# A fused attention and two-MoE kernel: 32-bit low words, fewer filler products, another table of urgencies

## The chip, the cores and the metric

The kernel runs on one core of a Trainium2 chip. A core has TensorE (PE in the profile, with PEld for its weight loads), VectorE (DVE), ScalarE (ACT), GpSimd (POOL) and SyncE (SP), which here issues all transfers. The metric is the device time of one execution in microseconds; lower is better.

## The reference

Three stages follow each other. The first is an attention of 4 batches, 8 heads, 576 tokens and head size 64 (a band of seven neighbours, plus an attention on tokens averaged by four); its result is a matrix x of 2304 tokens by 512. Two layers with weights follow:

```python
x = transpose(attn_out).reshape(2304, 512)
x = ((x @ w_a) * (x @ w_b)) @ w_out          # d_ff 1536
h = x @ w_in2                                # d_ff 2048
g = maximum(h, 0) + alpha * minimum(h, 0)
out = (g @ w_out2).astype(float32)
```

The weights arrive in eight bytes each (float64 bits); q, k, v are float32.

## The kernel before

Every matmul of the layers uses fp16 pairs: a number is split into a high and a low fp16 word after scaling by a power of two, and three products (high·high, high·low, low·high) are added in PSUM.

The work is cut into steps: `s1(j, f)` makes the 128 hidden columns f of layer 1 for the 288 tokens of block j (24 products of 288 columns, into two of the four PSUM banks m0 to m3), `s2(j, d)` the second half of layer 1 (36 products), `s3` and `s4` the same for layer 2 in blocks of 384 tokens. Blocks 0 and 1 of s1 are interleaved, four steps to each chunk of weights; block 1 needs tile 5, the last of batch 0. The PE steps of s1 to s4 form one chain with a fixed order. Around the chain lie the attention tiles (`turn`, `soft`, `p_turn`, `av_t`, 24 of them; `x_add` writes a tile's fp16 pair into xt) and the preparation of the weights, all on shared buffers: the tile zone holds attention data first and weights of layer 2 later, wo and x2s hold raw weights first.

After each s1 step ACT copies one bank to tm, DVE multiplies it with the other bank (`tm<-m,tm`), ACT makes the high word (`gt<-tm`) and DVE the low one (`gt<-gt,tm`); s2 reads gt. After s2, DVE adds two banks into x2s (`x2s<-m,tm`).

`narrow` turns a raw tile of eight-byte weights into float32 in four passes: ACT scales the low 32-bit word of each weight to a small count and writes it back over the raw tile, DVE puts two bits of the top word beside it (in the orders `TENSOR_SCALAR wo<-wo` or `zone<-zone`, 16-bit), DVE shifts the high word into the destination (`TENSOR_SCALAR wab<-wo`), and POOL adds the two. `cols_bound` (ACT), `top_of` (PE, DVE: tr, td) and `cols_split` (ACT and DVE, after us_ab and ws) then give scaled fp16 pairs. There are 48 raw tiles: 20 of 1024 weights per partition (12 of w_a and w_b, 8 of w_in) and 28 of 512 (w_out of both layers). Raw tiles of w_a and w_b are loaded into three places in turn.

A planner sets the order of every engine's instructions before anything is issued. `Plan.cost` gives each instruction an estimated duration, `reschedule` runs a list schedule in which the ready instruction of highest urgency goes first, and the table URGENT shifts the urgency of groups of steps by hand. `fill` then looks at each gap that the plan shows on PE in its first 200 us and puts constant products (identity by identity, 128x256, `m<-idf`) into 0.7 of it. An engine runs its instructions strictly in the issued order.

Of the kernel before, what the change touches and what calls it, by code (L numbers as in the profile page):

```python
# [12 lines left out]
U32 = mybir.dt.uint32  # L13
# [12 lines left out]
class Plan:  # L26
# [66 lines left out]
    def cost(self, eng, method, out, ins, kw):  # L93
        n = self.free(out)
        if eng == self.PE:
            if method == "transpose":
                n = self.free(out)
                w = 2 if ins[0].dtype == F32 else 1
            else:
                w = 4 if ins[0].dtype == F32 else 1  # L100
            return max(0.03, n * w * 0.000425)
        m = max([n] + [self.free(a) for a in ins])
        if eng == self.POOL:
            return 0.2 + m * (0.0026 if method == "tensor_tensor" else 0.0011)
        if eng == self.ACT:
            if ins and ins[0].dtype == U32:
                return 0.2 + 0.00243 * m
            return 0.2 + 0.0009 * m + (0.19 if kw.get("accum_out") is not None else 0)
        if out.dtype == I16:
            return 0.1 + 0.00144 * m  # L110
        if method in ("tensor_scalar", "tensor_copy", "memset", "tensor_scalar_mul"):
            return 0.12 + 0.0009 * m
        return 0.14 + 0.0011 * m
# [130 lines left out]
    def fill(self, t0, t1, chain, early, stat, mov, each):  # L244


        pe = [o for o in self.order if o.eng == self.PE]
        f = self.nc.tensor.matmul
        add = []
        for a, b in zip(pe, pe[1:]):  # L250
            n = int(0.7 * (b.start - a.end) / each)
            if n < 2 or not t0 <= a.end < t1:
                continue
            g = next(o for o in chain if o.start >= b.start)
            if g is chain[0]:
                out = early
            else:
                if not g.calls[0][2]["start"] or any(p.end > a.end - 0.5 for p in g.preds if p.eng in (self.DVE, self.ACT)
                                                     and p.name[:2] in ("s1", "s2")):
                    continue  # L260
                out = g.calls[0][1][0]
            o = self.new(self.PE)
            o.calls = [(f, (out[:, :mov.shape[1]], stat, mov), dict(start=True, stop=True))] * n
            o.start, o.end = a.end + 1e-6, b.start
            o.name, o.n = "fill", -1
            add.append(o)
        self.order = sorted(self.order + add, key=lambda o: o.start)
# [11 lines left out]
def kernel(  # L279
# [24 lines left out]
    def V(method, *a, **kw):  # L304
        P("vector", method, *a, **kw)

    def A(method, *a, **kw):
        P("scalar", method, *a, **kw)

    def G(method, *a, **kw):  # L310
        P("gpsimd", method, *a, **kw)
# [151 lines left out]
    def narrow(raw, dst):  # L463


        w = raw.bitcast(I32).rearrange("p (n t) -> p n t", t=2)
        h = raw.bitcast(I16).rearrange("p (n t) -> p n t", t=4)
        A("activation", out=h[:, :, 0], in_=raw.bitcast(U32).rearrange("p (n t) -> p n t", t=2)[:, :, 0],
          func=ACTF.Copy, scale=2.0 ** -29)
        V("tensor_scalar", out=h[:, :, 1], in0=h[:, :, 3], scalar1=-0x4000, scalar2=None, op0=ALU.bitwise_and)  # L470
        d = dst.bitcast(I32)
        V("tensor_scalar", out=d, in0=w[:, :, 1], scalar1=3, scalar2=0x3FFFFFFF,
          op0=ALU.logical_shift_left, op1=ALU.bitwise_and)
        G("tensor_tensor", out=d, in0=d, in1=w[:, :, 0], op=ALU.add)
# [20 lines left out]
    def rows_narrow(t, i, n, raw):  # L495
        narrow(raw, slot(t, i))
        A("activation", out=raw.bitcast(BF16)[:, :DM], in_=slot(t, i), func=ACTF.Square, accum_out=row_ss[n][:, i:i + 1])
# [17 lines left out]
    def cols_words(t, i, raw):  # L515
        narrow(raw, slot(t, i))
# [646 lines left out]
    for n, i in enumerate((3, 4, 5)):  # L1163
        t = head_end + 4 * n
# [36 lines left out]
    for i in range(3, NTILE):  # L1201
        b, t = divmod(i, TPB)
# [37 lines left out]
    def group(name):  # L1240
        kind = name.rstrip("0123456789")
        n = name[len(kind):]
        if kind in ("turn", "bound", "soft", "pturn", "av", "v", "x", "load") and n:
            b = int(n) // TPB
            return f"{kind}@{b}" if kind in ("x", "load") else f"t@{b}" if b else f"t0@{n}"
        if name[:3] in ("s1_", "s2_"):
            return f"{name[:2]}@{name[3]}"
        return kind if kind in ("wow", "wos", "wo2w", "wo2s") else name


    URGENT = {"alphas": -35, "bs0": -60, "bs1": -115, "bs2": 15, "bs3": -25, "gexp0": -45, "gexp1": -90,
# [13 lines left out]

    cal.sort(key=lambda x: x[:2])
    for _, _, fn, P.name, bias, P.rel in cal:
        P.bias = bias + URGENT.get(group(P.name), 0.0)
        fn()
# [35 lines left out]
```

## Time and profile before

| | us |
|---|---|
| median of 3 runs (lowest to highest) | 1039.46 (1034.23 to 1042.77) |
| the profiled execution | 1042.84 |
| span in the profile, first to last instruction | 1041.1 |
| PE busy, share of the span | 1004.1, 96% |
| DVE busy | 611.7, 59% |
| ACT busy | 512.1, 49% |
| POOL busy | 140.4, 13% |

The profiled execution took 1.7 us more than its span and is the slowest of the four times. Constant products count as PE busy, so PE's 96% is more than its useful share.

### The profile page before, as it was taken

How to read it: one execution, taken by the hardware profiler on the slowest of the kernel's cores; microseconds unless marked ns; L12 is line 12 of the kernel's file. 1: busy time of each engine (PE TensorE's matmuls, PEld its weight loads, DVE VectorE, ACT ScalarE, POOL GpSimd, SP SyncE). 2: the span in 40 equal slices, each digit the busy share in tenths (PEclk: the TensorE clock that was granted, in tenths of full speed). 3: DMA queues.
4: the chain of work that ended last, by engine and by line, in shares of the span. 5: the costliest groups of instructions: out<-in, count | busy, mean ns of one | idle time of the engine just before them, and what ended most of it. 6: DMA issues, size and time to landing. Idle time of an engine off the chain costs nothing.

```text
span 1041.1 us, 18632 instructions
## 1 busy us (share of the span) xinstructions
PE 1004.1 (96%) x7631; PEld 694.1 (67%) x7631; DVE 611.7 (59%) x1245; ACT 512.1 (49%) x967; POOL 140.4 (13%) x128
## 2 busy tenths in 40 slices
PE   8889799989999999999979999999999999999998
PEld 5677577768787787887756777654645555454553
DVE  5899998857656866567868777540514415042240
ACT  3677688544333444345666775451615426062350
POOL 2345742002200020000244120000000000000000
PEclk9889999989999999999989999999999999999999
DMA  9674551014310063111561421010010200000000
GB/s 161 227 210 145 148 142 34 1 26 85 70 48 1 23 108 91 25 65 42 163 220 41 128 82 47 2 31 31 1 51 11 64 21 21 30 12 11 21 1 31
DMA packets 95942, 69.50 MB, mean 67 GB/s; under 512 B 71152, under 2 KB 78704, under 8 KB 95856
## 3 DMA queue, kind: packets, MB, share of 16 engines
q1 hardware_dynamic: 95856, 68.31, 24.8%
q8 instruction: 60, 0.98, 0.4%
q14 instruction: 26, 0.21, 0.1%
HBM read 58.86 MB, written 9.44 MB: 66 GB/s over the span
## 4 chain that ended last, share of the span: by engine, by line
PE 84%; DVE 8%; SPq 2%; ACT 2%; issue 2%; DMA 1%; POOL 1%; POOLq 0%; DVEq 0%
PE m L272 74%; PE a L272 8%; SPq L272 2%; DVE zone L272 2%; DVE wo L272 2%; DVE wab L272 1%; DMA zone<-in_v_dram 1%; PE r L272 1%; ACT zone L272 1%; ACT wo L272 1%; POOL zone L272 1%; DVE xt L272 0%; DVE ws L272 0%; DVE gm L272 0%; DVE gn L272 0%
## 5 line engine op out<-in xcount | busy, mean ns | idle before, releaser
L272 PEld LDWEIGHTS <-wab 128*128 128x128 f16 x3168 | 307.8, 98 | 164.0 <-issue 6.4
L272 PE MATMUL m<-xt,wab 128*128 128x288 f16 x2304 | 297.4, 287 | 4.9 <-DVE tm L272 2.3
L272 DVE SCALAR_TENSOR_TENSOR gt<-tm,nal,tm 128x384 f32<-128x384 f32 x96 | 59.3, 618 | 220.8 <-ACT tm L272 220.8
L272 PE MATMUL m<-xt,zone 128*128 128x384 f16 x1152 | 188.5, 326 | 0.0
L272 PE MATMUL m<-zone,wab 128*128 128x512 f16 x864 | 187.5, 379 | 0.0
L272 PEld LDWEIGHTS <-zone 128*128 128x128 f16 x1152 | 112.6, 98 | 74.8
L272 ACT ACTIVATE tm<-m 128x384 f32<-128x384 f32 (+1 forms) x224 | 97.5, 477 | 105.7 <-PE m L272 102.9
L272 PEld LDWEIGHTS <-wo 128*128 128x128 f16 x1152 | 112.2, 99 | 38.7 <-issue 9.2
L272 POOL TENSOR_TENSOR zone<-zone 72x256 f32<-72x256 f32 (+2 forms) x60 | 77.6, 1301 | 390.3 <-DVE zone L272 178.5
L272 PE MATMUL m<-gt,wo 128*128 128x288 f16 x864 | 114.1, 291 | 7.6 <-DVE gt L272 5.5
L272 ACT ACTIVATE zone<-zone 96x832 f32<-96x832 f32 (+5 forms) x73 | 81.7, 1150 | 31.5 <-DVE zone L272 24.9
L272 ACT ACTIVATE gt<-m,uf 128x512 f32<-128x512 f32 x18 | 12.4, 687 | 164.8 <-PE m L272 164.8
L272 PE MATMUL a<-zone 64*96 64x104 f32 (+4 forms) x1104 | 76.7, 272 | 4.9 <-DVE zone L272 3.8
L272 PEld LDWEIGHTS a<-zone 64*96 64x96 f32 (+4 forms) x1104 | 62.1, 155 | 22.9 <-issue 15.2
L272 ACT COPY zone<-a 104x384 f32<-104x384 f32 (+4 forms) x124 | 53.8, 476 | 40.7 <-PE a L272 40.3
L272 ACT COPY tm<-m 128x288 f32<-128x288 f32 x96 | 38.8, 404 | 67.5 <-PE m L272 64.1
L272 DVE SCALAR_TENSOR_TENSOR tm<-m,tm 128x288 f32<-128x288 f32 x96 | 43.5, 454 | 38.3 <-PE m L272 33.0
L272 DVE SCALAR_TENSOR_TENSOR wab<-gt,kap,wab 128x384 f16<-128x384 f32 x96 | 58.8, 614 | 8.3 <-ACT wab L272 8.3
L272 ACT ACTIVATE wab<-gt,kap 128x384 f16<-128x384 f32 x96 | 59.0, 616 | 1.5 <-DVE gt L272 1.5
L272 PE MATMUL m<-idf 128*128 128x256 bf16 x375 | 53.2, 293 | 0.0
L272 PE MATMUL a<-idf,zone 96*104 96x96 f32 (+4 forms) x392 | 42.8, 249 | 5.3 <-DVE zone L272 4.2
L272 ACT ACTIVATE gt<-tm 128x288 f16<-128x288 f32 x72 | 31.7, 443 | 32.0 <-DVE tm L272 31.7
(172 smaller groups left out, 948.0 us busy)
## 6 DMA issues: line engine op xcount, KB each, us to landing
zone<-in_moe_w_out_dram SPq DMA_DIRECT2D x16, 512.0 KB
zone<-in_moe_w_in_dram SPq DMA_DIRECT2D x8, 1024.0 KB
wo<-in_moe_w_a_dram SPq DMA_DIRECT2D x6, 1024.0 KB
wo<-in_moe_w_b_dram SPq DMA_DIRECT2D x6, 1024.0 KB
x_d<-x2s SPq DMA_DIRECT2D x8, 576.0 KB
out_dram<-gt SPq DMA_DIRECT2D x18, 256.0 KB
zone<-in_k_dram SPq DMA_DIRECT2D x21, 208.0 KB
zone<-in_v_dram SPq DMA_DIRECT2D x21, 208.0 KB
```

What stands on the lines that cost most here:

```text
L272: f(*args, **kw)
```

## The change

Four edits. The ACT pass of `narrow` writes its count as a 32-bit word in place of a 16-bit one, at the same step of eight bytes (DVE's bits overwrite the upper half afterwards, as before). The planner's price for that pass falls, 0.00243 to 0.00095 us an element. `fill` uses 0.3 of a gap in place of 0.7 where the gap begins before 30 us of plan time. The table URGENT has other numbers throughout.

```diff
             if ins and ins[0].dtype == U32:
-                return 0.2 + 0.00243 * m
+                return 0.2 + 0.00095 * m
...
-            n = int(0.7 * (b.start - a.end) / each)
+            n = int((0.3 if a.end < 30.0 else 0.7) * (b.start - a.end) / each)
...
-        A("activation", out=h[:, :, 0], in_=raw.bitcast(U32).rearrange("p (n t) -> p n t", t=2)[:, :, 0],
+        A("activation", out=w[:, :, 0], in_=raw.bitcast(U32).rearrange("p (n t) -> p n t", t=2)[:, :, 0],
           func=ACTF.Copy, scale=2.0 ** -29)
...
-    URGENT = {"alphas": -35, "bs0": -60, "bs1": -115, "bs2": 15, "bs3": -25, "gexp0": -45, "gexp1": -90,
+    URGENT = {"alphas": 35, "bs0": 120, "bs1": -20, "bs2": -30, "bs3": -10, "gexp0": -60, "gexp1": 95,
```

`h` is the raw tile seen as 16-bit words (four to a weight), `w` the same as 32-bit words (two to a weight).

The first place is DVE in the preparation of the first chunk of weights, around the reading of its scale from PSUM (`us_ab<-r`); x2s and nz there belong to the softmax of tile 2, `wo<-wo` is the bits' pass of the fourth raw tile. DVE before:

```order
L272 TENSOR_REDUCE tr_119<-r_70 2x1
L272 TENSOR_TENSOR x2s<-a_67,nm_125 96x416
L272 TENSOR_SCALAR td_121<-idf,tr_119 2x2
L272 TENSOR_SCALAR wab<-wo 128x1024
L272 TENSOR_SCALAR us_ab<-r_70 128x2
L272 TENSOR_SCALAR alp<-a_174 128x16
L272 TENSOR_SCALAR us_ab<-us_ab 128x2
L272 TENSOR_SCALAR wo<-wo 128x1024
L272 TENSOR_REDUCE nz_127<-x2s 96x8
```

DVE now:

```order
L272 TENSOR_REDUCE tr_119<-r_70 2x1
L272 TENSOR_TENSOR x2s<-a_67,nm_125 96x416
L272 TENSOR_SCALAR td_121<-idf,tr_119 2x2
L272 TENSOR_SCALAR wo<-wo 128x1024
L272 TENSOR_REDUCE nz_127<-x2s 96x8
L272 TENSOR_SCALAR us_ab<-r_70 128x2
```

The bits' pass and the softmax's sum now stand ahead of the reading of the scale, the shift behind it. On ACT at the same place (x2s is the exponential of tile 2, `zone<-a` that of the pooled attention), before:

```order
L272 ACTIVATE wo<-wo 128x1024
L272 ACTIVATE zone<-a_68 72x432
L272 ACTIVATE x2s<-x2s 96x832
L272 ACTIVATE zone<-a_69 72x432
L272 ACTIVATE wo<-wo 128x1024
```

And ACT now:

```order
L272 ACTIVATE wo<-wo 128x1024
L272 ACTIVATE x2s<-x2s 96x832
L272 ACTIVATE zone<-a_68 72x432
L272 ACTIVATE zone<-a_69 72x432
L272 ACTIVATE wo<-wo 128x1024
```

The exponential of tile 2, on which the softmax's sum waits, has moved ahead of the pooled one.

The second place is the end of s1 of block 5 and the start of its s2, while the raw tiles of layer 2 (zone, 1024 and 512) are narrowed. ACT before:

```order
L272 COPY tm_86<-m_63 128x288
L272 ACTIVATE gt<-tm_89 128x288
L272 ACTIVATE xt<-xt_109,sx_169 128x4x96
L272 ACTIVATE zone<-zone 128x1024 x2
L272 ACTIVATE zone<-zone 128x512 x2
L272 COPY tm_87<-m_65 128x288
L272 ACTIVATE gt<-tm_88 128x288
```

ACT now:

```order
L272 ACTIVATE gt<-tm_88 128x288
L272 COPY tm_87<-m_65 128x288
L272 ACTIVATE xt<-xt_109,sx_169 128x4x96
L272 ACTIVATE zone,rm_93<-zone 128x512
L272 ACTIVATE xt<-zone,sx_169 128x4x96
L272 ACTIVATE gt<-tm_89 128x288
L272 ACTIVATE xt<-zone,sx_169 128x4x96
L272 ACTIVATE zone,rm_93<-zone 128x512
L272 ACTIVATE zone<-zone 128x1024 x2
```

The last high word of gt now stands ahead of the counts of those raw tiles. On DVE there, before:

```order
L272 TENSOR_SCALAR zone<-zone 128x1024 x2
L272 TENSOR_SCALAR zone<-zone 128x512
L272 TENSOR_SCALAR zone<-zone 128x1024
L272 TENSOR_SCALAR zone<-zone 128x512 x3
L272 SCALAR_TENSOR_TENSOR tm_89<-m_66,tm_87 128x288
L272 SCALAR_TENSOR_TENSOR gt<-gt,tm_88 128x288
L272 SCALAR_TENSOR_TENSOR gt<-gt,tm_89 128x288
```

DVE now:

```order
L272 SCALAR_TENSOR_TENSOR tm_89<-m_66,tm_87 128x288
L272 SCALAR_TENSOR_TENSOR xt<-xt_109,sx_169,xt 128x4x96
L272 SCALAR_TENSOR_TENSOR gt<-gt,tm_88 128x288
L272 SCALAR_TENSOR_TENSOR xt<-zone,sx_169,xt 128x4x96
L272 SCALAR_TENSOR_TENSOR gt<-gt,tm_89 128x288
L272 SCALAR_TENSOR_TENSOR xt<-zone,sx_169,xt 128x4x96
L272 TENSOR_SCALAR zone<-zone 128x1024 x4
L272 TENSOR_TENSOR x2s<-m_63,tm_86 128x288
```

The last low words of gt have moved from behind the passes over zone to ahead of four of them; the first sum of s2 (`x2s<-m,tm`) stands behind these four.

## Rows read from the trace of the kernel before

**Rows 1.** The page, part 1: busy time and share of the span.

```profile
PE 1004.1 (96%) x7631; PEld 694.1 (67%) x7631; DVE 611.7 (59%) x1245; ACT 512.1 (49%) x967; POOL 140.4 (13%) x128
```

**Rows 2.** Busy time by stretch: PE, PEld, DVE, ACT, POOL, granted clock, DMA.

```profile
0.00:121.00 121.00, 101.78 (x901) 78.89 (x902) 103.34 (x179) 73.67 (x93) 54.19 (x65) 0.90 0.73 186
121.00:167.00 46.00, 45.90 (x435) 36.79 (x435) 44.25 (x88) 37.44 (x72) 21.00 (x15) 1.00 0.47 113
...
500.00:600.00 100.00, 89.12 (x705) 68.64 (x704) 78.32 (x137) 68.30 (x114) 35.30 (x19) 0.95 0.46 144
```

**Rows 3.** The timeline of PE: rows with idle time, start and length first.

```profile
120.96 5.92 PE L272 MATMUL m<-xt,wab 128*128 128x288 f16 x47 [1.93 <-DVE xt L272]
...
526.72 0.28 PE L272 MATMUL m<-gt,wo 128*128 128x288 f16 x1 [2.10 <-ACT gt L272]
531.89 0.88 PE L272 MATMUL m<-gt,wo 128*128 128x288 f16 x3 [4.88 <-DVE gt L272]
...
558.88 1.37 PE L272 MATMUL m<-xt,wab 128*128 128x288 f16 x9 [2.33 <-DVE tm L272]
```

**Rows 4.** Groups of instructions by form: busy us, mean ns, idle before.

```profile
L272 ACT ACTIVATE wo<-wo 128x1024 int16<-128x1024 uint32 x12 | 30.1, 2510 | 0.0
L272 ACT ACTIVATE zone<-zone 128x512 int16<-128x512 uint32 x16 | 21.3, 1363 | 1.9 <-DMA zone<-in_moe_w_out_dram 1.9
L272 ACT ACTIVATE wab<-wab 128x1024 bf16<-128x1024 f32 x12 | 12.6, 1056 | 5.3 <-DVE wab L272 3.3 <-POOL wab L272 2.0
L272 DVE TENSOR_SCALAR wo<-wo 128x1024 int16<-128x1024 int16 x12 | 16.9, 1412 | 0.1
L272 DVE TENSOR_SCALAR wab<-wo 128x1024 int32<-128x1024 int32 x12 | 9.9, 827 | 0.0
```

**Rows 5.** The constant products: their group by form, then two timeline rows of PE.

```profile
L272 PE MATMUL m<-idf 128*128 128x256 bf16 x375 | 53.2, 293 | 0.0
...
5.12 1.27 PE L272 MATMUL m<-idf 128*128 128x256 bf16 x5
18.66 0.71 PE L272 MATMUL m<-idf 128*128 128x256 bf16 x5
```

**Rows 6.** Timelines of ACT, DVE and POOL, 29 to 51 us.

```profile
29.97 2.51 ACT L272 ACTIVATE wo<-wo 128x1024 int16<-128x1024 uint32 x1
...
32.51 1.33 DVE L272 TENSOR_SCALAR wo<-wo 128x1024 int16<-128x1024 int16 x1
...
33.93 2.68 POOL L272 TENSOR_TENSOR wab<-wab,wo 128x1024 int32<-128x1024 int32 x1 [25.54 <-DVE wo L272]
...
35.41 1.24 DVE L272 TENSOR_SCALAR gn<-gm 72x8 bf16<-72x8 f32 x1
38.78 2.00 DVE L272 TENSOR_TENSOR gn<-gr,gn 72x8 bf16<-72x8 f32 x1
40.70 0.17 DVE L272 TENSOR_SCALAR gn<-gm 72x8 bf16<-72x8 f32 x1
49.45 0.16 DVE L272 TENSOR_SCALAR us_ab<-r 128x2 f32<-128x2 f32 x1 [3.13 <-PE r L272]
49.73 1.32 DVE L272 TENSOR_SCALAR wo<-wo 128x1024 int16<-128x1024 int16 x1
50.85 0.98 DVE L272 TENSOR_REDUCE nz<-x2s 96x8 f32<-96x832 f32 x1
```

**Rows 7.** The timeline of DVE where PE's wait at 120.96 us ends.

```profile
120.30 0.60 DVE L272 SCALAR_TENSOR_TENSOR xt<-zone,sx,xt 128x384 f16<-128x384 f32 x1
120.83 0.67 DVE L272 TENSOR_REDUCE vst<-zone 104x1 f32<-104x512 f32 x1
```

**Rows 8.** Timelines of ACT and DVE from 518 us, and one stretch by engine.

```profile
518.99 7.12 ACT L272 ACTIVATE zone<-zone 128x1024 int16<-128x1024 uint32 x4
...
523.85 6.30 DVE L272 TENSOR_SCALAR zone<-zone 128x1024 int16<-128x1024 int16 x4 [0.73 <-ACT zone L272]
...
530.00:540.00 10.00, 7.53 (x47) 5.22 (x47) 6.04 (x9) 5.86 (x11) 5.13 (x3) 0.70 0.74 224
```

25 rows, old and new, of the table URGENT are left out of this document.

## The prediction

> **What bounds the kernel now.** I read the page's busy shares first: PE 96% [rows 1]. That looks like a kernel in which no other engine can give anything, but part of it is filler: 375 constant products, 53.2 us [rows 5]; in the issued order 349 of them stand before block 1's first product and 26 behind it. So I next asked from when PE is dense, by the timeline of its waits and by the busy time of stretches. Up to 121 us DVE is busy 103 of 121 us and PE's 102 contain nearly all of the filler; from 121 to 167 us PE is busy 45.90 of 46 at the full clock [rows 2]. The wait that ends there, at 120.96, is for xt of tile 5 [rows 3], which DVE finishes at 120.90 [rows 7]. So one term is when DVE gets tile 5 done; what follows is PE's own work, which the change leaves as it is, plus its later waits. The large ones lie together: 2.10 us on ACT's gt, 4.88 on DVE's gt and 2.33 on DVE's tm, between 526 and 559 us [rows 3]. Only 89 of 100 us are busy there [rows 2]; from 530 to 540 the granted clock is 0.70 [rows 8]. ACT and DVE have slack over the whole span (49 and 59%), so what they save counts at these two places only.
>
> **Terms.** They are made against the profiled execution of 1042.84 us, 1.7 over its span of 1041.1 and 3.4 above the median of 1039.46; the sum is applied to both.
>
> *The price of a count.* Now 2.51 us for 1024 and 1.36 for 512 [rows 4]. No row shows ACT writing 32-bit words at a step of eight bytes. The floor is ACT's pass from 32 to 16 bits at a step without gaps, 1.06 for 1024 [rows 4]; the ceiling is the present 2.51. Which is nearer? DVE reads 32-bit words at that same step in 0.83, and is slower, 1.41, where it reads and writes 16-bit words at it [rows 4]. So the step alone is cheap, and the narrow word is what goes with the slow rows. I take 1.1 and 0.65. Summed over 20 and 28 passes that is 20 x 1.41 + 28 x 0.71 = 48 us of ACT, hidden but for the terms below.
>
> Here a page speaks against the change. The Trainium skill, SBUF — State Buffer, section "Door 1: The DMA port swizzle (why `[64,N]` ≈ `[32,N]`)", describes lines of 16 bytes, with full bandwidth from two hits in a line on. By that, two- and four-byte words at a step of eight cost the same, and nothing would be gained. But by the same rule the present pass, with two hits in a line, should run at full bandwidth, and the row does not agree: 2510 ns against 1056.
>
> *The head, up to 121 us.* (a) The first count stands alone: DVE's bits begin at 32.51, when ACT's pass from 29.97 is done, and POOL's add of that tile follows at 33.93 [rows 6]. A count of 1.1 starts this chain 1.4 us earlier. (b) At 49.45 DVE waits 3.13 us for PE's r before us_ab. After it come the bits of the fourth tile, 1.32, and the softmax's sum, 0.98 [rows 6]. In the new order these two stand ahead of us_ab, and the shift that stood there goes behind it. What the two need comes earlier: the exponential has moved ahead of the pooled one, and counts are shorter. So 2.3 us of the 3.13 is filled with work. (c) Ahead of the sixth xt stand about 1.6 us less of DVE's work: one vst of 0.67 [rows 7], a shift of 512 (half of 0.83) and three short operations like the one of 0.17 [rows 6]. I count half, 0.8, since something must be ready in their place. Sum 1.4 + 2.3 + 0.8 = **-4.5 us**. The bounds: 0, if DVE's work only closes up to meet other waits (it is busy almost without a pause from 50 us on), and -9, twice the sum, if the shorter counts save a stop of the same size at the second chunk.
>
> *Fewer constant products in the first gaps.* The issued order has 20 in these gaps in place of 60, 311 in all in place of 375. They cost nothing in idle time; their other effect is on the clock. At 5.12 us five take 1.27 us, 0.25 each, the lower level of 1.2 GHz; at 18.66 five take 0.71, 0.14 each, 2.4 GHz [rows 5]. If PE rises later, the real products before 30 us go on at half speed, though most of these are waited for by DVE in any case. I take **+1**, from -1 (fewer products in the way of real ones) to +4.
>
> *Behind 121 us.* The order has 17 constant products there in place of 26: 9 x 0.14 = **-1**.
>
> *The stop at 526 us.* From 518.99 ACT runs four counts in a row, 7.12 us, and DVE four bits' passes from 523.85, 6.30 us [rows 8]. The last gt stood behind them; PE's s2 waited 2.10 and then 4.88 for it [rows 3]. In the new order the last high words stand ahead of the two long counts on ACT and the last low words ahead of the passes on DVE, so they come as fast as PE's own s1 lets them. I leave 3 of these 7 us for the last copy, product, high and low word, which must run after the last product of s1: -4. With no such stop the clock should not fall to 0.70; that was worth 0.3 x 7.53 = 2.3 us [rows 8], of which I take 2. Sum **-6**. But the four long passes do not vanish: they now stand ahead of the first sum of s2 (x2s), and 4 x 1.41 = 5.6 us of DVE [rows 4] stand before a PSUM bank is given free. A bank is needed again after two steps of s2, so this can return as a wait; the 2.33 at 559 may also stay or grow. Bounds -12 (all three waits and the clock) and +3 (the wait moves to the bank, the clock falls as before).
>
> Sum: -4.5 + 1 - 1 - 6 = -10.5. On the median that is **1029.0**; on the profiled execution 1032.3.
>
> **Rivals.**
> *The price doesn't fall*, because the uint32 source or the step of eight bytes sets it. For it: no row separates source and width on ACT. Against it: DVE's rows. Then (a) goes, the counts arrive late for (b), and on ACT at 519 us there are still 7 us of counts; the reordered gt saves perhaps 2. Some -2.5: 1037. Chance 0.15.
>
> *POOL's adds hold DVE up more (slower).* DVE's tiny passes over gn take 0.17 us alone, but 1.24 and 2.00 beside adds of POOL; the first ends at 36.65, as the add does (33.93 + 2.68 = 36.61) [rows 6]. So an add stopped DVE for 1.07 and 1.83 us of its 2.68, 1.45 on average; twelve adds of this size lie in the head, 17 us of DVE's time there. The new order and the shorter counts shift all of them. If each met a DVE instruction at its start, 12 x (2.68 - 1.45) = 15 us would be added, and the sum would be +4.5: 1044. It decides from an average of 2.3 us on (1.45 + 10.5/12), where the gain is gone. Against it: DVE's instructions of 1 us and more cover part of any add, in the old order as in the new. Chance 0.10. The Trainium skill, SBUF — State Buffer, section "Who interferes with whom", says that DVE and GpSimd share a pair of ports as an exclusive lock, which whoever issued first holds for the whole instruction; the trace agrees (36.65 against 36.61). By that rule it is the order of issue that decides, so the risk can't be excluded.
>
> *PE stays at 1.2 GHz* through the first 30 to 45 us, for want of the 40 products. The real products between 10 and 30 us (about 12.7 us at the higher level, by the timeline of PE) would take twice that, less 40 x 0.14 = 5.7 us freed: some +6, and the sum is about -4.5: 1035. For it: the clock is 0.90 over the head even now [rows 2]. Against it: DVE, not PE, sets the pace there. Chance 0.10.
>
> *Both places clear entirely:* -9 in the head, -11 at 526, no loss of clock: 1020. Chance 0.10.
>
> **How the numbers follow.** The forecast has 0.55, the rivals 0.15, 0.10, 0.10 and 0.10. Within 1% (10.4 us), about what a measurement of this kernel can tell from no change, lies everything above 1029; the forecast stands at that line, so it counts half as faster. Faster: 0.55 x 0.6 + 0.10 + a twentieth from the others = 0.48; slower by over 1%: the second rival at its end and part of unforeseen queues, 0.09; within: 0.43. The forecast's own range goes from 1020 to 1036. It is widened to 1015 by the bounds at 526 us and to 1042 by the unchanged price and the milder part of the second rival, which leaves out 2 in 10.
>
> **What will show it.** In the changed profile the count's group should read about 1.1 us for 1024 and 0.65 for 512 (2.5 is the first rival). DVE's us_ab should have no wait of 3 us; PE's last long wait for xt should end near 116 us; at the start of s2 of block 5 there should be no wait of 4.88 on gt, and the clock there should be above 0.9. If instead PE waits for a PSUM bank given free by x2s, behind four passes on zone, the stop has only moved. Tiny DVE passes of over 2 us beside POOL's adds show the second rival, products of the first 30 us at 0.25 the third. The forecast is wrong as a whole if the head doesn't shorten: then -6 is all, and 1034 the time; and it is wrong upward if new waits come up in layers where PE is now dense, which a new table for all steps can bring and no row of before shows.

## The result, and the profile after

The changed kernel takes 1027.18 us (median of 4 runs, 1026.16 to 1028.36), the kernel before 1040.64 beside it: a ratio of 0.9881, with a 95% interval of 0.9834 to 0.9928. The forecast was 1029.0, with 1015 to 1042 as its range. The profiled execution has a span of 1024.1 us, 17.0 less than before; more than the medians' 13.5, because the profile of before was of one of the longer runs and this one of a shorter.

The page's first part, of the changed kernel (it answers to [rows 1]):

```profile
PE 990.5 (97%) x7567; PEld 684.1 (67%) x7567; DVE 607.5 (59%) x1245; ACT 471.0 (46%) x967; POOL 137.4 (13%) x128
```

ACT lost 41 us and DVE 4, while PE is as full as before. The groups by form answer to [rows 4, 5]; columns are busy us, mean ns and the idle time ahead:

```profile
L272 DVE TENSOR_SCALAR wo<-wo 128x1024 int16<-128x1024 int16 x12 | 21.5, 1794 | 0.4 <-ACT wo L272 0.3
L272 ACT ACTIVATE wo<-wo 128x1024 int32<-128x1024 uint32 x12 | 13.9, 1157 | 0.4 <-DMA wo<-in_moe_w_b_dram 0.4
L272 ACT ACTIVATE zone<-zone 128x512 int32<-128x512 uint32 x16 | 10.7, 674 | 2.4 <-DMA zone<-in_moe_w_out_dram 2.4
...
L272 PE MATMUL m<-idf 128*128 128x256 bf16 x311 | 41.8, 280 | 0.0
```

The count takes 1157 and 674 ns in place of 2510 and 1363. But DVE's passes over wo are longer than before, 1794 ns in place of 1412. They do the same work; they stand still in between, which is taken up below.

By stretch (PE, PEld, DVE, ACT, POOL, granted clock, DMA; it answers to [rows 2, 8]):

```profile
0.00:121.00 121.00, 98.68 (x918) 76.90 (x920) 108.46 (x190) 60.64 (x104) 60.90 (x69) 0.96 0.75 192
...
500.00:600.00 100.00, 94.27 (x751) 73.56 (x746) 85.78 (x142) 60.41 (x125) 37.91 (x21) 0.97 0.46 153
530.00:540.00 10.00, 10.00 (x84) 8.00 (x82) 9.94 (x13) 6.88 (x10) 5.62 (x2) 1.00 0.52 165
540.00:550.00 10.00, 4.81 (x25) 3.07 (x23) 9.90 (x11) 3.36 (x8) 6.01 (x3) 0.66 0.00 0
```

And PE's rows that answer to [rows 3], start and length first:

```profile
112.77 5.92 PE L272 MATMUL m<-xt,wab 128*128 128x288 f16 x47 [1.51 <-DVE xt L272]
...
524.80 1.63 PE L272 MATMUL m<-gt,wo 128*128 128x288 f16 x12 [0.43 <-DVE x2s L272]
...
545.37 4.94 PE L272 MATMUL m<-xt,wab 128*128 128x288 f16 x24 [5.19 <-DVE tm L272]
```

Two of DVE's rows that answer to [rows 6]:

```profile
29.79 1.33 DVE L272 TENSOR_SCALAR wo<-wo 128x1024 int16<-128x1024 int16 x1
...
45.46 0.14 DVE L272 TENSOR_SCALAR us_ab<-r 128x2 f32<-128x2 f32 x1
```

PE is dense from 112.77 on (from there it waits seldom and briefly), 8.2 us earlier. The stop at 526 us is gone, and 530 to 540 runs at the full clock. In its place PE waits 5.19 us on tm at 545, and there the clock falls to 0.66. So of the 17.0 us between these two profiles, 8.2 lie in the head and 8.8 behind it. Behind it PE's idle time went from 17.8 to 11.3 us (6.4) and its busy time from 902.4 to 900.0 (2.4: nine constant products fewer and less time at the lower clock).

### The profile page after: what moved, and what is told of

Its sections match the earlier page's. It is cut to its first block, busy times and chain, and to the rows that moved or that the text cites. A ratio compares the mean times of both kernels' runs of the same rounds, so it can differ in the third digit from the quotient of the medians.

```text
span 1024.1 us, 18490 instructions
## 1 busy us (share of the span) xinstructions
PE 990.5 (97%) x7567; PEld 684.1 (67%) x7567; DVE 607.5 (59%) x1245; ACT 471.0 (46%) x967; POOL 137.4 (13%) x128
## 4 chain that ended last, share of the span: by engine, by line
PE 85%; DVE 10%; SPq 2%; DMA 1%; issue 1%; ACT 1%; DVEq 0%
PE m L272 74%; PE a L272 10%; DVE zone L272 4%; DVE wo L272 2%; SPq L272 2%; DMA zone<-in_v_dram 1%; DVE xt L272 1%; PE r L272 1%; DVE wab L272 1%; DVE nm L272 1%; DVE nz L272 1%; DVE gm L272 0%; ACT zone L272 0%; DVE gn L272 0%; DVE tm L272 0%
## 5 line engine op out<-in xcount | busy, mean ns | idle before, releaser
L272 ACT ACTIVATE gt<-m,uf 128x512 f32<-128x512 f32 x18 | 12.4, 687 | 161.7 <-PE m L272 161.7
L272 ACT ACTIVATE zone<-zone 96x832 f32<-96x832 f32 (+5 forms) x73 | 61.4, 847 | 38.7 <-DVE zone L272 31.4
L272 DVE TENSOR_SCALAR zone<-zone 128x512 int16<-128x512 int16 (+3 forms) x48 | 46.5, 1009 | 3.9 <-PE a L272 2.4
```

The lines of the kernel that those rows point to most:

```text
L272: f(*args, **kw)
```

## The experiments

**Each edit alone.** The first set takes price and order apart. The write alone, in the old order:

```diff
-        A("activation", out=h[:, :, 0], in_=raw.bitcast(U32)...
+        A("activation", out=w[:, :, 0], in_=raw.bitcast(U32)...
```

> The kernel before with the 32-bit write alone: every engine's order, the price in the plan and the 375 constant products stay. Theory 'both' (price and order each bring part): the counts take 1.16 and 0.67 us as in the changed kernel; the first chunk's bits start 1.35 us earlier, and at 526 us the four counts in a row take 3.7 in place of 7.12 us, so the waits of 2.10 and 4.88 on gt shrink to about 3 to 4 together; some -5 us, ratio about 0.995. Theory 'order' (the gain is the table's, ACT is off the path): ratio 0.998 to 1.002, waits at 526 us within 1 us of before. Theory 'price' (all of it is the count): ratio 0.988, dense PE from 113 us on.

1041.27 us, ratio 1.0008 (0.9994 to 1.0022). The counts are as cheap as in the changed kernel, 1154 ns, and nothing comes of it. The timelines of ACT, DVE and PE at the stop, in this kernel:

```profile
514.67 3.33 ACT L272 ACTIVATE zone<-zone 128x1024 int32<-128x1024 uint32 x4
...
516.99 9.11 DVE L272 TENSOR_SCALAR zone<-zone 128x1024 int32<-128x1024 int32 x7
525.90 0.48 DVE L272 SCALAR_TENSOR_TENSOR tm<-m,tm 128x288 f32<-128x288 f32 x1
...
527.84 0.88 PE L272 MATMUL m<-gt,wo 128*128 128x288 f16 x3 [6.79 <-DVE gt L272]
```

ACT is done by 518.0. But seven passes on DVE, 9.11 us without a pause, still stand ahead of the product tm and the last gt. (A timeline row that joins several passes shows the form of the first; these are bits' passes and shifts of 1024 and of 512.) PE's 2.10 on ACT and 4.88 on DVE [rows 3] have become one wait of 6.79 on DVE: the queue that DVE runs in order was the bound, and ACT only the first to be seen in it. In the head the first bits' pass starts at 31.21 in place of 32.51 [rows 6], as term (a) says, and PE is dense 1.3 us earlier, from 119.69; the runs' median doesn't show it.

The reverse, the changed kernel with the 16-bit write (the diff above, turned round):

> The changed kernel with the 16-bit write put back; its order, planned price and 311 constant products stay. Theory 'both': the counts take 2.51 and 1.36 us, which this order has not planned for; head 3 to 6 us longer than the changed kernel (dense PE from 116 to 119 us), about 1033 to 1036 us, ratio 0.993 to 0.996 to the kernel before. Theory 'order': as the changed kernel, 0.988. Theory 'price': as before or slower, 1.000 to 1.005.

1034.7 us, ratio 0.9943 (0.9928 to 0.9958). So the order (new table and lower planned price, with fewer early constant products) brings 5.9 us without the cheap count, and the cheap count some 6.5 more in this order, by the ratios, against none in the old. The interval of 0.9881 touches this one at 0.9928; two further runs with the cheap count in nearly this order, below, lie clear of it at 0.9870 and 0.9888. PE is dense from 116.61 here, and waits 2.68 us on x2s at 527.88, the bank behind four long passes that the prediction names as a risk; with the short count that wait is 0.43.

The new table alone, and the other way round the old table with all other edits (in each the planner orders anew):

```diff
-    URGENT = {"alphas": -35, "bs0": -60, "bs1": -115, ...
+    URGENT = {"alphas": 35, "bs0": 120, "bs1": -20, ...
```

> The kernel before with the new table of urgencies alone: 16-bit write, the old price in the plan, 0.7 of every gap filled. Theory 'pair' (the table is worth something only in the order that it makes with the lower planned price; write alone gave 1.0008 and the old table with the rest 1.0019): ratio 0.996 to 1.006, with waits at 520 to 570 us as large as before. Theory 'table' (the new numbers are better at any price): 0.990 to 0.995, as the changed kernel with the 16-bit write (0.9943).

1045.33 us, ratio 1.0058 (1.0037 to 1.0079): slower than before.

> The changed kernel with the old table of urgencies: 32-bit write, the plan's lower price and fewer early constant products stay, so the planner orders anew with the old numbers. Theory 'both': about half of the gain, 1032 to 1036 us, ratio 0.992 to 0.996. Theory 'order' (the new table brings it): 0.998 to 1.004. Theory 'price': 0.988. A table that is tuned to one price may fit another badly, so a ratio above 1.004 would say that the old numbers hurt with the new price.

1042.91 us, ratio 1.0019 (1.0007 to 1.0030). PE's rows of the two around the end of block 5, first the new table alone, then the old table with the rest:

```profile
529.39 15.67 PE L272 MATMUL m<-gt,wo 128*128 128x288 f16 x113 [3.36 <-DVE gt L272]
...
562.42 4.75 PE L272 MATMUL m<-xt,wab 128*128 128x288 f16 x24 [2.72 <-DVE tm L272]
569.47 4.77 PE L272 MATMUL m<-xt,wab 128*128 128x288 f16 x24 [2.30 <-DVE tm L272]
```

```profile
533.68 8.78 PE L272 MATMUL m<-gt,wo 128*128 128x288 f16 x48 [5.27 <-DVE x2s L272]
...
563.15 4.77 PE L272 MATMUL m<-xt,wab 128*128 128x288 f16 x24 [4.01 <-DVE tm L272]
```

In both PE still waits at these places, and between 500 and 600 us it is as busy as before (88.90 and 89.13 in place of 89.12). Their heads end earlier than in the profile of before, at 117.57 and 116.11, but by less than single executions of one order differ (below). Behind it they take 925.9 and 925.1 us in place of 920.1; part of that are waits elsewhere, such as 2.23 us on gn near 217 us in both (at most 0.8 before) and 2.53 on x2s near 418 with the old table. Numbers of urgency and planned price belong together: neither gains anything without the other.

**The constant products.** The rule of 0.7 for all gaps, in the changed kernel:

```diff
-            n = int((0.3 if a.end < 30.0 else 0.7) * (b.start - a.end) / each)
+            n = int(0.7 * (b.start - a.end) / each)
```

> The changed kernel with 0.7 of every gap filled, 351 constant products in place of 311, the first gaps with 60; nothing else moves on any engine. Theory 'filler is idle time': within 2 us of the changed kernel, ratio 0.986 to 0.990. Theory 'clock' (fewer early products cost the clock): 3 us faster, 0.985, with real products before 30 us at the higher level earlier. Theory 'in the way' (they delay real products): 3 us slower, 0.991.

1025.67 us, ratio 0.9870 (0.9851 to 0.9890): as the changed kernel. And none at all (the call of fill left out):

> The changed kernel without any constant products (311 of them, 42 us of PE, left out; they compute nothing that is used). Theory 'idle filler': within 3 us of 1027, ratio 0.985 to 0.990. Theory 'clock': PE's clock stays at the lower level in much of the first 120 us, its real work there of some 60 us takes up to 30 us more in part behind DVE's work, 1032 to 1045 us. Theory 'in the way': 1020 to 1025.

1030.13 us, ratio 0.9904 (0.9881 to 0.9927). The head in four stretches of this kernel (PE first, the clock after POOL):

```profile
0.00:30.00 30.00, 20.95 (x130) 12.50 (x130) 18.49 (x39) 10.85 (x21) 7.75 (x44) 0.94 1.03 190
30.00:60.00 30.00, 24.30 (x191) 19.11 (x189) 29.04 (x49) 16.84 (x25) 15.36 (x6) 0.58 0.69 220
60.00:90.00 30.00, 18.83 (x117) 13.77 (x118) 26.20 (x53) 12.10 (x20) 12.80 (x7) 0.51 0.90 234
90.00:121.00 31.00, 18.16 (x142) 13.37 (x141) 29.69 (x44) 17.67 (x31) 21.12 (x12) 0.67 0.41 119
```

The clock is at its lower level for most of 30 to 121 us, and that costs little: 3 us by the medians, and the intervals of 0.9904 and 0.9881 overlap. DVE, busy 103 of 121 us, sets the pace by these rows, and PE's slower products mostly fit beside it.

**What holds DVE up.** A kernel that leaves out the reference's work and times single operations:

> Leaves out the reference's whole computation and writes zeros and eight words to the output; measures ACT passes of 128x1024 by form, and DVE operations issued while an add of POOL runs. Theory 'narrow word': 16-bit words written at a step of eight bytes cost 2.5 us whether the source has gaps or not, 32-bit words at that step 1.1 to 1.2, 16-bit words without gaps 1.1. Theory 'step of the source': every form that reads at eight bytes costs more than 2 us when it writes 16 bits, packed or not, and the packed source writes 16-bit words at eight bytes in 1.1. Theory 'conversion': 16-bit integers cost 2.5 in any layout. For POOL's add (2.4 us alone): tiny scale operations and the bits' pass of DVE behind its start wait for its end (over 2 us for a pass that takes 0.2 or 1.3 alone), the reduction and the operation with two tensors do not; a theory of shared bandwidth would stretch all of them alike.

ACT's groups by form in it (other and raw have a step of eight bytes, dst as int16 from raw one of four; dst as int32 and pk are packed):

```profile
L288 ACT ACTIVATE other<-raw 128x1024 int16<-128x1024 uint32 x2 | 4.9, 2456 | 0.0
L288 ACT ACTIVATE other<-pk 128x1024 int16<-128x1024 uint32 x2 | 4.9, 2444 | 0.0
...
L288 ACT ACTIVATE dst<-raw 128x1024 int16<-128x1024 uint32 x2 | 2.7, 1326 | 0.0
...
L288 ACT ACTIVATE other<-raw 128x1024 int32<-128x1024 uint32 x2 | 2.2, 1099 | 0.1
L288 ACT ACTIVATE dst<-pk 128x1024 int32<-128x1024 uint32 x2 | 2.1, 1035 | 0.0
```

The source makes no difference (2456 and 2444). A 16-bit word at eight bytes is dear, at four bytes 1326, and a 32-bit word at eight bytes costs nearly what a packed one does. DVE's timeline in the same kernel, first two operations alone, then three of which each follows the start of a POOL add of 2.37 us (from 53.00, 61.25 and 69.52 us), and the last of these adds:

```profile
38.20 1.27 DVE L347 SCALAR_TENSOR_TENSOR lo<-big,st,hi 128x1024 f16<-128x1024 f32 x1
39.39 0.16 DVE L350 TENSOR_SCALAR sb<-st 128x8 bf16<-128x8 f32 x1
...
53.43 3.10 DVE L344 TENSOR_SCALAR raw<-raw 128x1024 int16<-128x1024 int16 x1
...
61.69 3.02 DVE L347 SCALAR_TENSOR_TENSOR lo<-big,st,hi 128x1024 f16<-128x1024 f32 x1
...
70.07 1.85 DVE L350 TENSOR_SCALAR sb<-st 128x8 bf16<-128x8 f32 x1
...
69.52 2.37 POOL L338 TENSOR_TENSOR dst<-dst,raw 128x1024 int32<-128x1024 int32 x1 [1.76 <-DVE dst L336]
```

Alone they take 1.30, 1.27 and 0.16 us. Beside an add the tiny one ends at 71.92, the add at 71.89; the others run from the add's end on. That the operation with two inputs would not wait, as was expected, was wrong. Reductions, 0.65 us alone, don't wait: two of them in a row beside an add take 1.40 together. So the row of gn [rows 6] was no exception: an add stops DVE's scale, bits and two-input operations for the rest of its length, and, as the rows at 537 us below show, its shift.

How much that is worth: the 48 adds on 8 columns only (nearly all low words are left out of the weights), the order of every engine kept, first in the changed kernel. The lines stand behind the planning.

```diff
+    for o in P.order:
+        if o.eng == P.POOL and o.calls[0][0].__name__ == "tensor_tensor" and o.calls[0][2]["out"].dtype == I32:
+            f, ar, kw = o.calls[0]
+            o.calls[0] = (f, ar, dict(kw, out=kw["out"][:, :8], in0=kw["in0"][:, :8], in1=kw["in1"][:, :8]))
```

> The changed kernel with POOL's 48 additions of the low words done for 8 of 1024 or 512 columns only, in the same order on every engine; so nearly all low words are left out of the weights, and the split sees the high words alone. Theory 'POOL holds DVE' (an add of 2.4 us stops DVE's two-port operations for all of its length): DVE's passes return to their lengths alone (bits 1.30, shift 0.68, the scale of two columns 0.17), dense PE starts 4 to 8 us earlier than 112.8, the wait of 5.2 us on tm near 545 us falls below 1.5; 1012 to 1018 us, ratio 0.973 to 0.979. Theory 'DVE's own work' (the stalls fall in DVE's idle time): dense PE within 2 us of 112.8, the wait at 545 over 4, 1023 to 1027 us.

1001.14 us, ratio 0.9633 (0.9615 to 0.9652), a larger gain than the 1012 to 1018 us that were expected of a POOL that holds DVE. The page's first part, and the row of PE from which it is dense:

```profile
PE 983.8 (98%) x7567; PEld 680.4 (68%) x7567; DVE 562.7 (56%) x1245; ACT 470.5 (47%) x967; POOL 65.8 (7%) x128
...
97.95 6.28 PE L272 MATMUL m<-xt,wab 128*128 128x288 f16 x48
```

With the same instructions DVE is busy 562.7 in place of 607.5 us: 45 us of its busy time were standing, at the least, since the short adds still take time (1.03 us each on wo). PE is dense 14.8 us earlier, so most of the gain lies in the head. The wait on tm is gone. The same in the kernel before:

> The kernel before with POOL's 48 additions of low words done for 8 columns only, in the same order on every engine; nearly all low words are left out of the weights. The same in the changed kernel gave 1001 us, 26 less. Theory 'add sets both' (what the change saves and what the adds cost are separate): also some 26 us less, 1011 to 1017 us, ratio 0.972 to 0.978. Theory 'the change lets the adds bite' (its shorter counts bring DVE's passes up against POOL's adds, so more stands still): only 10 to 15 us less, 1024 to 1030. Theory 'before suffers more': below 1005, and then the two kernels would be equal without the adds.

1009.58 us, ratio 0.9705 (0.9683 to 0.9728), a little below the 1011 to 1017 expected; DVE is busy 565.8 us. DVE's and PE's rows of this kernel at the stop (the first answers to the 6.30 us of [rows 8], the last two to the waits of [rows 3]):

```profile
500.81 3.10 DVE L272 TENSOR_SCALAR zone<-zone 128x1024 int16<-128x1024 int16 x4 [0.73 <-ACT zone L272]
...
504.11 1.05 DVE L272 SCALAR_TENSOR_TENSOR gt<-gt,tm 128x288 f16<-128x288 f16 x2
...
503.69 0.28 PE L272 MATMUL m<-gt,wo 128*128 128x288 f16 x1 [0.83 <-ACT gt L272]
504.61 5.42 PE L272 MATMUL m<-gt,wo 128*128 128x288 f16 x41 [0.63 <-DVE gt L272]
```

The four passes that took 6.30 us take 3.10, the two low words of gt behind them 1.05 in place of 2.95, and PE's waits for gt, 2.10 and 4.88 before, are 0.83 and 0.63, in the old order and with the 16-bit count. PE is dense from 100.70 us on, in place of 120.96. The adds cost 31 us before and 26 after, by the ratios. Without them the change is still worth some 7.5 us, with them 12.4; the second has an interval of 5 us to either side, so whether the adds are part of the change's gain is open.

By groups of form in the kernel before, from 523.8 to 529.9 us, two of those four passes:

```profile
L272 DVE TENSOR_SCALAR zone<-zone 128x1024 int16<-128x1024 int16 x1 | 2.7, 2706 | 0.7 <-ACT zone L272 0.7
L272 DVE TENSOR_SCALAR zone<-zone 128x512 int32<-128x512 int32 x1 | 2.6, 2579 | 0.0
```

The four are one bits' pass of 1024, a shift of 512 and two bits' passes of 512; the two shown stood beside adds (POOL's from 522.95 and 526.64 us), and alone take 1.30 and about 0.4 (0.41 in the same kernel at 512.92).

**The new wait at 545 us.** DVE's and POOL's timelines of the changed kernel ahead of it:

```profile
537.05 4.11 DVE L272 TENSOR_SCALAR zone<-zone 128x1024 int32<-128x1024 int32 x2
540.96 1.25 DVE L272 SCALAR_TENSOR_TENSOR zone<-zone,ws 128x1024 f16<-128x1024 f32 x1
542.13 2.91 DVE L272 TENSOR_SCALAR zone<-zone 128x512 int16<-128x512 int16 x1
544.85 0.47 DVE L272 SCALAR_TENSOR_TENSOR tm<-m,tm 128x288 f32<-128x288 f32 x1
...
536.17 3.22 POOL L272 TENSOR_TENSOR zone<-zone 128x1024 int32<-128x1024 int32 x1 [3.64 <-DVE zone L272]
541.24 3.21 POOL L272 TENSOR_TENSOR zone<-zone 128x1024 int32<-128x1024 int32 x1 [1.85 <-DVE zone L272]
```

A pass over 512 weights, 0.74 us where no add runs, takes 2.91 beside the add from 541.24. The row of 4.11 is a shift, 0.68 alone, that takes 2.89 beside the add from 536.17, and a bits' pass of 1.29 behind it. The product that PE waits for stands behind them. Moving it ahead of the split and the pass (DVE's order):

```diff
+ SCALAR_TENSOR_TENSOR tm<-m,tm 128x288
+ SCALAR_TENSOR_TENSOR gt<-gt,tm 128x288
  SCALAR_TENSOR_TENSOR zone<-zone,ws 128x1024
  TENSOR_SCALAR zone<-zone 128x512
- SCALAR_TENSOR_TENSOR tm<-m,tm 128x288
  TENSOR_SCALAR zone<-zone 128x512 x3
- SCALAR_TENSOR_TENSOR gt<-gt,tm 128x288
```

> The changed kernel with one place of DVE's order altered: near 545 us the product tm and the low words of gt stand ahead of a split and of four passes over 512 weights, and two of POOL's adds follow their passes. Theory 'queue' (PE's wait of 5.19 us is tm's place behind these): the wait goes below 1.5 us and the granted clock of 540 to 560 us rises from 0.83 to above 0.9; 4 to 7 us faster, 1020 to 1023 us, ratio 0.981 to 0.984. Theory 'backlog' (DVE has too much to do there in any order): a wait of 3 to 5 us comes back within the next two steps of s1, 1025 to 1028 us.

1027.45 us, ratio 0.9888 (0.9865 to 0.9912): no gain, as the theory of a backlog had it. PE in this kernel:

```profile
547.62 3.10 PE L272 MATMUL m<-xt,wab 128*128 128x288 f16 x24 [1.30 <-DVE tm L272]
553.60 0.37 PE L272 MATMUL r<-idf,wm 128*2 128x128 f32 x1 [2.88 <-ACT zone L272]
554.65 5.48 PE L272 MATMUL m<-xt,wab 128*128 128x288 f16 x24 [0.68 <-DVE tm L272]
```

The wait on tm shrank from 5.19 to 1.30 us, and 2.88 and 0.68 came up behind it, the first for the bound of the next weights (r), which stands in PE's order and hangs on the passes and adds that were moved back. The place has too much for DVE and POOL to do; order only chooses who waits. In this profile PE was dense from 118.43 us on, in an unchanged order of the head, against 112.77 (and from 116.32 with 0.7 of all gaps filled): the head of single executions differs by some 5 us, so shares of the head read from one profile are good to that only.

**Taking the add off POOL.** If the adds are the cost, DVE can join the words itself, in two passes with two inputs:

```diff
-        V("tensor_scalar", out=h[:, :, 1], in0=h[:, :, 3], scalar1=-0x4000, scalar2=None, op0=ALU.bitwise_and)
         d = dst.bitcast(I32)
-        V("tensor_scalar", out=d, in0=w[:, :, 1], scalar1=3, scalar2=0x3FFFFFFF,
-          op0=ALU.logical_shift_left, op1=ALU.bitwise_and)
-        G("tensor_tensor", out=d, in0=d, in1=w[:, :, 0], op=ALU.add)
+        V("scalar_tensor_tensor", out=w[:, :, 0], in0=w[:, :, 1], scalar=3, in1=w[:, :, 0],
+          op0=ALU.logical_shift_left, op1=ALU.bitwise_or)
+        V("scalar_tensor_tensor", out=d, in0=w[:, :, 1], scalar=0x3FFFFFFF, in1=w[:, :, 0],
+          op0=ALU.bitwise_or, op1=ALU.bitwise_and)
```

> The changed kernel with the add taken off POOL: DVE joins count and shifted word by two passes with two inputs (shift and or, then or and and), in place of bits, shift and POOL's add; a count of 8 that meets a set bit loses its carry, and weights of 2 or more would not be read rightly. The table of urgencies stays, the planner orders anew. DVE has 2 x 1.27 us for 1024 in place of 1.30 + 0.68, 19 us more in all, and no add to stand for. Theory 'POOL holds DVE': the stops cost more than 19 us, and the chain from count to bound is 2.4 us shorter per tile: 1012 to 1024 us. Theory 'DVE's own work sets the head': 5 us slower or more, 1030 to 1040. A table made for another plan can add some 10 us to either.

1022.04 us, ratio 0.9822 (0.9797 to 0.9848), with a table that was made for other operations. And with one made for these by the planner's own estimate, other numbers throughout:

```diff
-    URGENT = {"alphas": 35, "bs0": 120, "bs1": -20, ...
+    URGENT = {"alphas": -135, "bs0": -200, "bs1": -130, ...
```

> The same as the run before it, with a table of urgencies found anew for these operations by the planner's own estimate. Theory 'POOL holds DVE': 1008 to 1020 us, ratio 0.969 to 0.981, faster than both kernels; DVE's passes at their lengths alone, no wait of PE above 3 us behind 121 us. Theory 'DVE's own work': 1025 to 1035.

1001.32 us, ratio 0.9637 (0.9611 to 0.9662): 26 us below the changed kernel, a larger gain than the 1008 to 1020 us expected, and the fastest of all that compute the reference. Its first part and the two groups of new passes over wo:

```profile
PE 980.1 (98%) x7536; PEld 677.8 (68%) x7536; DVE 583.8 (58%) x1245; ACT 470.4 (47%) x967; POOL 43.3 (4%) x80
...
L272 DVE SCALAR_TENSOR_TENSOR wo<-wo 128x1024 int32<-128x1024 int32 x12 | 14.5, 1215 | 0.6 <-ACT wo L272 0.6
L272 DVE SCALAR_TENSOR_TENSOR wab<-wo 128x1024 int32<-128x1024 int32 x12 | 14.5, 1214 | 0.0
```

By their lengths the new passes give DVE more to do, 2 x 1.21 in place of 1.30 + 0.68; it is still busy 24 us less than in the changed kernel, since none of the 48 adds is there to stop it. Behind 95 us PE waits nowhere longer than 1.4 us. Not all of the 26 us is the add's: 5 came with the first version, 21 with the table, and no run says what such a search would give the changed kernel's own operations.

## Why the prediction was right

**The price** was right: 1.16 and 0.67 us against 1.1 and 0.65, and ACT is busy 41 us less where 48 were summed. The first rival, a price set by the source or the step, fell with the rows of the changed kernel, and the single forms show that on ACT it is the narrow word at a wide step that costs. That DVE's rows, from which the prediction took the price, differ for the same reason is not shown: those two passes differ in the step of their writes too, so part of this hit is luck. The page that spoke against it (the Trainium skill, SBUF — State Buffer, "Door 1: The DMA port swizzle (why `[64,N]` ≈ `[32,N]`)", by which two hits in a line of 16 bytes run at full bandwidth) does not agree with 2456 ns and 1099 ns at the same two hits in a line.

**The head** was forecast at -4.5 with bounds of 0 and -9. Its first two steps are there: the first bits' pass starts at 29.79 (1.4 of the 2.7 us by the order, since the write alone gives 31.21), and the wait of 3.13 for us_ab is gone (the row is at 45.46, with no wait, against 49.45); the third was not measured by itself. The one profile says -8.2. But by the profiles with the cheap count and this order of the head PE is dense from 112.77, 116.32 and 118.43 on, 2.5 to 8.2 us earlier than in the one profile of before, so a size of -4.5 agrees with them, and the whole of 8.2 can't be called the change's. The 16-bit write in this order, 116.61, lies among them. What is shown, by the ratios, is +0.8 us for the write alone, -5.9 for the order alone and -12.4 for both: the cheap count is worth some 6.5 us in the new order and nothing in the old; how that divides between the head and what follows is open. The prediction summed its terms as if each stood alone and has no such interplay.

**The stop at 526 us** was forecast at -6, "-4" of waits and "-2" of clock. From 500 to 600 us PE is busy 94.27 in place of 89.12, 5.2 us more, and the clock gave under 1, since its fall only moved, to 540 us: about right in size. But the place is a different one from the forecast's. The waits for gt went altogether (7 us where 4 were counted); the wait on tm, of which the text says that it "may also stay or grow", grew from 2.33 to 5.19. So the size is in part luck: two errors of some 3 us each, with opposite signs. Wrong was the thought that ACT's four counts were part of the cause: they went without any effect in the old order. Wrong, too, was the reading of the row of 6.30 us as four bits' passes of full length: half of it was standing beside POOL's adds (3.10 without them), as were two thirds of the 2.95 us of the last low words. The four passes that were to stand ahead of x2s, priced at 5.6 us, are two shifts and two bits' passes, 3.69 us in the changed kernel. DVE's place for gt, and so the new order, removed the stop; the cheap count then kept x2s from taking over (2.68 against 0.43).

**The constant products**: +1 for fewer early ones is not to be told from nothing (1025.67 with them, 1027.18 without); nine fewer behind 121 us were counted at -1, and PE's busy time there fell by 2.4 with less time at the lower clock in it. The third rival, the clock, has its effect but not its price: without any constant product the clock is 0.51 to 0.67 from 30 to 121 us and some 3 us are lost, not clear of noise, where the rival counted 6 for a smaller loss.

**POOL's adds**, the second rival, did not turn the change round, but its mechanism is the largest thing in this kernel. By the prediction's rows an add stopped DVE for 1.45 us on average, 17 us in the head. DVE's standing time over the whole span is 46 us before (611.7 - 565.8) and 45 after, so the change left it where it was: a little under 1 us for each of the 48 adds, less than the 1.45 that the prediction took from two. The rival was wrong in that the new order would raise it, and the prediction in treating it as a risk of the change only: at both places that it argued from, the queue on DVE was long because of it. With short adds in the kernel before the stop is 0.83 and 0.63 us in place of 2.10 and 4.88, and PE is dense at 100.70 in place of 120.96. The Trainium skill's rule of an exclusive lock (SBUF — State Buffer, "Who interferes with whom") agrees with 71.92 against 71.89 us, and its exception for reductions with the 1.40 us of two beside an add.

The forecast's chances hold one slip: the text lets 1029 count half as faster, and the sum takes 0.6.

Open stays how the 26 us of the adds divide into DVE's standing and the adds' own length in the chain from count to bound, 2.4 us for each tile: the runs with small adds take both away.

## What to carry to other kernels

When a wait names one engine, make that engine cheaper by itself before believing it: here 42 us less on ACT (512.1 to 470.1) moved nothing, since the queue behind it on DVE ended at nearly the same place. An order found for one set of prices is worth its time with these only, so price and order are measured together, and alone, before the gain is given to either. And an instruction much longer than its kind alone (0.17 against 1.24, 0.74 against 2.91) is the row to follow first: look at what another engine does in the same microseconds. A row that joins several instructions under one form hides such lengths, so take it apart before pricing it.

## What the runs showed that was not expected

- ACT writes 16-bit words at a step of eight bytes in 2.45 us for 128x1024, at four bytes in 1.33, and 32-bit words at eight bytes in 1.10, whatever the step of its source.
- 48 adds of POOL, 70 to 80 us of an engine that is busy 13% of the span, hold 45 us of DVE's time; the kernels are 26 and 31 us faster where they are short, and the largest part of that lies in the head (14.8 and 20.3 us).
- With PE at 1.2 GHz for most of 30 to 121 us (granted clock 0.51 to 0.67) the kernel loses some 3 us at most by the medians, beside a DVE that is busy 103 of 121 us.
